# One PSUM bank for the attention sums, one more for projections, and Exps shared by heads, in a pre-LN block with sliding attention and GEGLU

## The chip, the cores and the metric

The kernel runs on one core of a Trainium2 chip. The metric is the device time of one execution in microseconds. Times come from runs on the chip; the profile is one execution that the hardware profiler recorded. Engines are named as the profile names them: PE is TensorE, PEld its weight loader, DVE VectorE, ACT ScalarE, POOL GpSimd, SP SyncE, which issues the DMAs. PSUM has eight banks of 128 x 512 f32; products are summed there and read out by DVE or ACT.

## The reference

One transformer block on 2048 tokens of 448 features: attention with 16 heads of 28 over a window of 256 tokens, then a gated feed-forward part of width 1792. All inputs are f32.

```python
h  = x + softmax(mask(q @ k.T * 28 ** -0.5)) @ v @ wo    # q, k, v = split(layernorm(x) @ wqkv)
h2 = h + (gelu(n @ w_gate) * (n @ w_up)) @ w_down        # n = layernorm(h)
# mask: 0 <= i - j < 256
```

## The kernel before

**Tiles and blocks.** Tokens are cut into 16 tiles of 128 and 4 chunks of 512 (c); heads into 4 groups of 4 (g). One attention block is B = 4c + g: 4 heads by 512 query tokens. Its keys are the chunk's four tiles and the two tiles before them (m = 0 to 5; for c = 0 only 2 to 5). A key tile m meets 1, 2 or 3 query tiles (`parts`): 1 for m = 0 and 5, 2 for m = 1 and 4, 3 for m = 2 and 3.

**Stages.** `ln1` normalises a tile and turns it, `values` (L570) and `project_tile` (L622) make v, q and k as sums of 11 products each, with the operands split into a high and a low part. q and k go to DRAM and come back (`loads`, L654) in the layout in which each query row can also carry its maximum. A block then runs four steps:

- `scores`: 16 products (L672), and on DVE the masked row maximum of each (L676), two instructions.
- `maxima`: twice a block, the maxima are turned by a product (L703) and copied by ACT into extra rows of q (L349).
- `probs`: for each head and key tile one product (L744), keys by queries with the maximum already subtracted, then one Exp on ACT (L748) into the tile `pp`; `select` (L759) clears the masked corners on POOL.
- `attend`: the value products (L778), four heads packed side by side, in two halves (key tiles 0 to 2, then 3 to 5), summed over all six key tiles in a bank that must be zero at the start; `drain` turns the sum out of that bank (L812), divides it and splits it; `output` (L835) multiplies by wo and adds to the residual.

`ln2` and `feed_forward` (L984, L1008) follow. The first four of the 56 feed-forward products, the first two of them under the name `early`, may run before attention is over.

**Banks.** `allowed` says which bank a kind of product may take. Before the change the banks are: 0 and 1 scores, 2 and 3 probability products and turned maxima, 4 and 5 the attention sums of even and odd blocks (`("att", B % 2)`), 6 and 7 layer norms, values, projections and `output`; 7 also helps scores and probabilities once no projections are left.

**What sets the order.** The kernel is planned when it is built. Each function hands operations to `Lists.op` with an engine, a cost, a latency and a key; `Lists.run` plays them on a model of the engines, picks on each engine the lowest key among those that could start about now, assigns banks, and emits the instructions in that order. The chip then runs each engine's instructions strictly in the emitted order, and waits on semaphores. So a key or a cost does not change any instruction, only its place; and an instruction that waits holds all that is behind it on its engine, DMAs on SP included. Keys are counted in units of a block's 16: block B's scores stand at 16 B + 4 i + j, its probabilities `LAG_P` later, its value products `LAG_V` after the last of those, its projections `EDGE` before it.

Of the kernel before, what the change touches and what calls it, by code (L numbers as in the profile page):

```python
# [21 lines left out]
SCALE = float(DH) ** -0.5  # L22
# [12 lines left out]
LAG_T = 6  # L35
LAG_P = 15
LAG_V = 12
EDGE = 9
WIN = 14
FFN = 1000  # L40
LEAD = 30
# [7 lines left out]
LN1 = (0, -19, 55, 134)  # L49
LN2 = (166, 224)  # L50
VKEY = (-30, -23, 14, 24)
VHALF = 0
FETCH = 170
# [173 lines left out]
def block_kernel(ctx: ExitStack, tc, x, wqk_in, wv_in, wo_in, ffn_in, out):  # L227
# [335 lines left out]
    def values(t, p, n):  # L563
        key = 64 * (t // 4) + VKEY[t % 4] if t > 3 else 8 * t - 37 if not p else VHALF + 6 * t
        b = Bank("v")
        w = slice(224 * p, 224 * (p + n))
        c = slice(128 * col(t), 128 * col(t) + 128)
        for a in range(NP):
            h, wb, xb = TERMS[a]
            op("pe", mm(224 * n), 0.29 if n == 1 else 0.38, key + a / 16, lambda a=a, h=h, wb=wb, xb=xb: nc.tensor.matmul(  # L570
                bank[b.k][:, 0:224 * n], xT[:, xb, c], wv[:, h, wb, w], start=(a == 0),
                stop=(a == NP - 1)), [XT(col(t)), *(WV(p + i, h, wb) for i in range(n))], () if a else [V(t, p, n)], b, tag="v")
        op("act", 0.29 if n == 1 else 0.47, 0.39 if n == 1 else 0.57, key + 1, lambda: to_hi(
            v[:, at_v(t), 8 * p:8 * (p + n), 0:DH], bank[b.k][:, 0:224 * n].rearrange("p (h d) -> p h d", d=DH)),
           ["ones"], [V(t, p, n)], b)
# [35 lines left out]
    def project_tile(c, m):  # L611
# [6 lines left out]
        base = 16 * B - EDGE  # L618
# [117 lines left out]
    def probs(B, m, j, o):  # L736
        u = B % 2
        lo, hi = parts(m)
        n = (hi - lo + 1) * 128
        b = Bank("prob")  # L740
        key = 16 * B + LAG_P + ORDER[m] + j * n / 384

        def one():
            nc.tensor.matmul(bank[b.k][:, 0:n], rk[u][0:104, j, m * 128:m * 128 + 128],  # L744
                             rq[u][0:104, j, lo * 128:(hi + 1) * 128], start=True, stop=True)

        def exp():
            nc.scalar.activation(pp[:, j, o * 128:o * 128 + n], bank[b.k][:, 0:n], AF.Exp, scale=SCALE)  # L748
        q = [("rk", u, m), *(("pick", u, j) for j in range(4)), *((w, u, i) for i in range(lo, hi + 1) for w in ("rq", "rx"))]
        op("pe", mm(n), 0.19 + n / 2400, key, one, q, (), b, tag="prob")  # L750
        op("act", 0.065 + n * 0.00088, 0.16 + n * 0.00088, key, exp, (), pp_at(o, hi - lo + 1, j), b, tag="exp")
# [16 lines left out]
    def attend(B, ms, at):  # L768
        g, c = block(B)
        b = acc.setdefault(B, Bank(("att", B % 2)))  # L770
# [161 lines left out]
    def feed_forward():  # L932
# [3 lines left out]
        for gi, gn in enumerate(GROUPS):  # L936
            for c in range(4):
                down = [Bank(("down", i)) for i in range(4)]
                for k in range(gn):
                    i = sum(GROUPS[:gi]) + k  # L940
                    while loaded < 2:
                        loaded += 1
                        split += 1
                        weights(loaded, 16 * NB + 5 * loaded if loaded < 2 else FFN + 30 * first[loaded] - 20)
# [158 lines left out]
    def clear():  # L1103
        for i in range(2):
            b = Bank(("att", i))
            op("dve", 0.4, 0.5, 12 + i, lambda b=b: nc.vector.memset(bank[b.k], 0.0), (), ["cleared"], b, tag="clear",
# [17 lines left out]
    for c in range(CS):  # L1124
# [12 lines left out]
        for g in range(NG):  # L1137
# [11 lines left out]
            for half in ((0, 1, 2), (3, 4, 5)) if c else ((2, 3), (4, 5)):  # L1149
                for m in half:  # L1150
                    for j in range(4):
                        probs(B, m, j, at[m])
# [18 lines left out]
    def allowed(kind):  # L1171
# [3 lines left out]
        if kind in ("ln1", "v", "proj", "task", "ln2"):  # L1175
            return [6, 7] + ([5, 4] if left["clear"] else []) + \
                ([3, 2] if L.fresh("prob") or not left["prob"] else []) + \
                ([1, 0] if L.fresh("score") or not left["score"] else []) + \
                ([4, 5] if kind == "task" and not left["att"] else [])
# [4 lines left out]
        if kind == "early":  # L1184
            return [] if left["proj"] or left["v"] else [6] + ([] if left["score"] else [0, 1]) + \
# [8 lines left out]
        what, i = kind  # L1194
        if what == "att":
            return [4 + i]
        return [] if left["att"] or left["task"] or left.get("early") else [4 + i]
# [68 lines left out]
```

## Time and profile before

| | us |
|---|---|
| median of 3 runs (lowest, highest) | 727.81 (727.71, 727.92) |
| the profiled execution's own time | 727.88 |
| its span, first to last instruction | 726.2 |
| first score starts at | 40.7 |
| last score starts at | 301.3 |
| feed-forward products from about 336 to | 720 |

The profile's page cuts the span into 40 slices; the digits are tenths busy:

```profile
PE   8999999999999999999999999999999999999997
DVE  7968779978787769658464313244133234232224
ACT  7738777777867787786453222244222223222221
POOL 5504743544354446741000000000000000000000
DMA  8896867888548984342732000012100000001002
```

Each column is 18.2 us. To about the 18th column attention runs and all engines have much to do; behind it PE alone is full. The chain by line names what the time went to:

```profile
PE bank L984 53%; PE bank L622 10%; PE bank L744 6%; PE bank L672 6%; PE bank L778 5%; PE bank L570 5%; PE bank L835 5%; PE bank L1008 3%; DMA hres<-in_x_dram 1%; PE bank L404 1%; DVE mt L676 1%; PE bank L703 0%; ACT pp L748 0%; DVE hres L1086 0%; ACT xT L349 0%
```

L984 is the feed-forward part; L622, L744, L672, L778, L570 and L835 are attention's products.

In a row of instruction groups stand: line, engine, operation, output<-input, partitions x elements, count, then busy us and the mean ns of one, then the idle time of the engine before them and what ended it. A row of waits reads: engine, waiting instruction <- the one that ended the wait: total us, number, longest. A row of the timeline: start, us, engine, line, operation, count; neighbours of one kind are merged.

### The profile page before, as it was taken

The numbers are of one execution on the slowest core, as the hardware profiler recorded it, in microseconds if no ns is written. First come the engines' busy times: TensorE is split into PE (matmuls) and PEld (weight loads), VectorE is DVE, ScalarE is ACT, GpSimd is POOL, SyncE is SP. The second block draws the span as 40 slices with busy tenths as digits, with TensorE's granted clock in tenths as the row PEclk, the third lists the DMA queues.
The fourth block names the chain that finished last, engine by engine and source line by source line (L and its number), as shares of the span: only waits on it lengthen the run. The fifth ranks groups of instructions, "written<-read, shape, count | busy, mean of one in ns | idle before, by whom it ended". The sixth has DMA issues, their size and how long they took to land.

```text
span 726.2 us, 15085 instructions
## 1 busy us (share of the span) xinstructions
PE 717.8 (99%) x5732; PEld 594.4 (82%) x5732; DVE 401.4 (55%) x1067; ACT 366.4 (50%) x927; POOL 162.6 (22%) x285
## 2 busy tenths in 40 slices
PE   8999999999999999999999999999999999999997
PEld 7887778878787877778888888888888888888886
DVE  7968779978787769658464313244133234232224
ACT  7738777777867787786453222244222223222221
POOL 5504743544354446741000000000000000000000
PEclk9999999999999999999999999999999999999999
DMA  8896867888548984342732000012100000001002
GB/s 308 268 311 211 234 159 203 214 255 207 161 122 241 242 234 136 77 112 42 203 105 84 1 2 1 1 44 83 42 1 2 1 1 1 2 1 51 19 34 102
DMA packets 96929, 82.06 MB, mean 113 GB/s; under 512 B 41736, under 2 KB 83016, under 8 KB 96840
## 3 DMA queue, kind: packets, MB, share of 16 engines
q1 hardware_dynamic: 96712, 80.98, 38.5%
q8 instruction: 45, 0.74, 0.4%
q14 instruction: 28, 0.23, 0.1%
q10 hardware_dynamic: 144, 0.11, 0.0%
HBM read 50.27 MB, written 31.03 MB: 112 GB/s over the span
## 4 chain that ended last, share of the span: by engine, by line
PE 94%; DVE 2%; ACT 1%; issue 1%; DMA 1%; POOL 0%; SPq 0%; DVEq 0%; POOLq 0%
PE bank L984 53%; PE bank L622 10%; PE bank L744 6%; PE bank L672 6%; PE bank L778 5%; PE bank L570 5%; PE bank L835 5%; PE bank L1008 3%; DMA hres<-in_x_dram 1%; PE bank L404 1%; DVE mt L676 1%; PE bank L703 0%; ACT pp L748 0%; DVE hres L1086 0%; ACT xT L349 0%
## 5 line engine op out<-in xcount | busy, mean ns | idle before, releaser
L676 DVE CUSTOM_DVE_ANT_0 mt<-bank,mt 128x384 bf16<-128x384 f32 (+2 forms) x256 | 126.8, 526 | 29.0 <-PE bank L672 27.2
L748 ACT ACTIVATE pp<-bank 128x384 f32<-128x384 f32 (+2 forms) x352 | 122.5, 388 | 39.8 <-PE bank L744 36.8
L1050 DVE TENSOR_TENSOR mt<-bank,mt 128x512 f32<-128x512 f32 x54 | 37.1, 688 | 143.3 <-ACT mt L1048 143.3
L759 POOL TENSOR_SCALAR_AFFINE_SELECT pp<-pp 128x512 f32<-128x512 f32 x120 | 75.9, 646 | 107.6 <-ACT pp L748 86.3
L744 PE MATMUL bank<-rq,rk 104*128 104x384 f32 (+2 forms) x352 | 97.6, 303 | 0.6 <-ACT pp L748 0.2
L622 PE MATMUL bank<-xT 128*128 128x512 f32 x308 | 94.9, 400 | 0.0
L1048 ACT ACTIVATE mt<-bank 128x512 f32<-128x512 f32 x54 | 32.2, 596 | 118.0 <-PE bank L984 118.0
L984 PE MATMUL bank<-xT,rk 64*128 64x512 f32 x656 | 82.0, 388 | 0.0
L984 PE MATMUL bank<-xT,rec 64*128 64x512 f32 x656 | 81.9, 388 | 0.0
L672 PE MATMUL bank<-rk,rq 84*128 84x384 f32 (+2 forms) x256 | 80.8, 346 | 0.8 <-DVE mx L676 0.5
L744 PEld LDWEIGHTS bank<-rq,rk 104*128 104x128 f32 x352 | 65.0, 189 | 17.4 <-ACT pp L748 5.9
L984 PEld LDWEIGHTS bank<-xT,rk 64*128 64x128 f32 x656 | 63.0, 184 | 12.2
L984 PEld LDWEIGHTS bank<-xT,rec 64*128 64x128 f32 x656 | 63.0, 184 | 12.1
L1086 DVE TENSOR_TENSOR hres<-bank,hres 128x448 f32<-128x448 f32 (+1 forms) x65 | 35.7, 611 | 66.9 <-PE bank L984 64.8
L990 ACT ACTIVATE e<-bank 1x1 f32<-1x1 f32 x162 | 25.7, 158 | 81.2 <-PE bank L984 80.5
L984 PE MATMUL bank<-xT,proj 64*128 64x512 f32 x533 | 66.6, 388 | 0.0
L622 PEld LDWEIGHTS bank<-xT 128*128 128x128 f32 x308 | 55.4, 189 | 7.4 <-ACT v L349 0.4
L984 PEld LDWEIGHTS bank<-xT,proj 64*128 64x128 f32 x533 | 51.1, 184 | 9.9
L672 PEld LDWEIGHTS bank<-rk,rq 84*128 84x128 f32 x256 | 46.3, 189 | 12.2 <-DVE mx L676 5.2
L570 PE MATMUL bank<-proj,xT 128*128 128x448 f32 (+1 forms) x220 | 51.0, 337 | 0.2 <-ACT v L349 0.2
L778 PE MATMUL bank<-pp,v 128*29 128x384 f32 (+2 forms) x704 | 45.4, 388 | 0.0
L349 ACT ACTIVATE rq<-bank 8x512 fp32r<-8x512 f32 x64 | 37.5, 586 | 13.6 <-PE bank L703 12.6
(147 smaller groups left out, 1088.5 us busy)
## 6 DMA issues: line engine op xcount, KB each, us to landing
rk<-k SPq DMA_DIRECT2D x44, 336.0 KB
rq<-q SPq DMA_DIRECT2D x32, 336.0 KB
v<-in_ffn_dram SPq DMA_DIRECT2D x7, 736.0 KB
q<-proj SPq DMA_DIRECT2D x11, 448.0 KB
raw<-in_ffn_dram SPq DMA_DIRECT2D x6, 736.0 KB
xn<-xn SPq DMA_DIRECT2D x72, 56.0 KB
xT<-xn SPq DMA_DIRECT2D x20, 192.0 KB
hres<-in_x_dram SPq DMA_DIRECT2D x16, 224.0 KB
```

Of the source, the lines that this page charges most:

```text
L349: nc.scalar.activation(dst, src, AF.Copy)
L570: op("pe", mm(224 * n), 0.29 if n == 1 else 0.38, key + a / 16, lambda a=a, h=h, wb=wb, xb=xb: nc.tensor.matmul(bank[b.k][:, 0:224 * n], x ...
L622: op("pe", mm(512) + 0.002, 0.403, key, lambda a=a, h=h, wb=wb, xb=xb: nc.tensor.matmul(bank[b.k], wqk[m][:, h, wb, :], xT[:, xb, cc * 128 ...
L672: nc.tensor.matmul(bank[b.k][:, o:384], rq[u][0:3 * DH, j, i * 128:i * 128 + 128], rk[u][0:3 * DH, j, m0 * 128:(i + 3) * 128], start=True, ...
L676: nc.vector.tensor_tensor_reduce(junk[s % 2][:, o:384], bank[b.k][:, o:384], mask[:, o:384], 1.0, -BIG, OP.add, OP.max, mx[i // 2][:, i % ...
L744: nc.tensor.matmul(bank[b.k][:, 0:n], rk[u][0:104, j, m * 128:m * 128 + 128], rq[u][0:104, j, lo * 128:(hi + 1) * 128], start=True, stop=True)
L748: nc.scalar.activation(pp[:, j, o * 128:o * 128 + n], bank[b.k][:, 0:n], AF.Exp, scale=SCALE)
L759: nc.gpsimd.affine_select(a, a, pattern=[[0, 4], [-cm, 128]], compare_op=op_, fill=0.0, base=0, channel_multiplier=cm)
L778: nc.tensor.matmul(bank[b.k][32 * j:32 * j + DH + 1, lo * 128:(hi + 1) * 128], v[:, at_v(4 * c - 2 + m), 4 * g + j, :], pp[:, j, at[m] * 1 ...
L835: op("pe", mm(D), 0.38, wk, lambda a=a, h=h, oh=oh, wh=wh, i=i, k=k: nc.tensor.matmul(bank[k.k][:, 0:D], ohl[:, h, oh, i * 128:(i + 1) * 1 ...
L984: nc.tensor.matmul(bank[bk.k][:, 0:n], w, m, start=bool(start), stop=bool(stop), tile_position=(64 * x, 0), skip_group_check=True)
L1050: op("dve", 0.605, 0.702, key + 2 * NP, lambda: nc.vector.tensor_tensor(blocks(g2), src(1), blocks(g2), op=OP.mult), [*G2, *held[1]], G2, ...
```

## The change

Four things are done.

- **Banks.** All blocks sum their attention in one bank, 4. Bank 5 goes to layer norms, values, projections, `output` and `early` feed-forward products, beside 6 and 7. Only one bank is cleared at the start.
- **Shared Exps.** `probs` works on a key tile instead of a head: as many heads as fit into 512 columns share a bank and one Exp: one head of 384 columns, two of 256, four of 128. The probability products themselves keep their sizes. The cost that the planner takes for them is now `G * (n / 2400 + 0.009)`, where `mm(n)` had a floor of 0.115.
- **Keys.** `LAG_V` 12 to 10, `EDGE` 9 to 8 and another 4 for the last chunk (`ELAST`), `LEAD` 30 to 10, `LN1` and `LN2` for one chunk each, `FETCH` 170 to 210, another table of keys for the values of the last tile group (`VLAST`); `WKEY` writes out two numbers that were computed before.
- **Order.** All engines' orders change from these.

```diff
 LAG_T = 6
+VLAST = (-30, -25, 14, 24)
+ELAST = 4
+WKEY = (256, 261)
 LAG_P = 15
-LAG_V = 12
-EDGE = 9
+LAG_V = 10
+EDGE = 8
-LEAD = 30
+LEAD = 10
-LN1 = (0, -19, 55, 134)
-LN2 = (166, 224)
+LN1 = (0, -19, 55, 128)
+LN2 = (166, 231)
-FETCH = 170
+FETCH = 210
...
-        base = 16 * B - EDGE
+        base = 16 * B - EDGE - (ELAST if c == 3 else 0)
...
-    def probs(B, m, j, o):
+    def probs(B, m, o):
         n = (hi - lo + 1) * 128
-        b = Bank("prob")
-        key = 16 * B + LAG_P + ORDER[m] + j * n / 384
-
-        def one():
-            nc.tensor.matmul(bank[b.k][:, 0:n], rk[u][0:104, j, m * 128:m * 128 + 128],
-                             rq[u][0:104, j, lo * 128:(hi + 1) * 128], start=True, stop=True)
-
-        def exp():
-            nc.scalar.activation(pp[:, j, o * 128:o * 128 + n], bank[b.k][:, 0:n], AF.Exp, scale=SCALE)
+        G = 512 // n
+        for j in range(0, 4, G):
+            b = Bank("prob")
+            key = 16 * B + LAG_P + ORDER[m] + j * n / 384
+
+            def some(j=j, b=b):
+                for i in range(G):
+                    nc.tensor.matmul(bank[b.k][:, n * i:n * i + n], rk[u][0:104, j + i, m * 128:m * 128 + 128],
+                                     rq[u][0:104, j + i, lo * 128:(hi + 1) * 128], start=True, stop=True)
+
+            def exp(j=j, b=b):
+                nc.scalar.activation(pp[:, j:j + G, o * 128:o * 128 + n],
+                                     bank[b.k][:, 0:G * n].rearrange("p (g t) -> p g t", g=G), AF.Exp, scale=SCALE)
...
+            cost = G * (n / 2400 + 0.009)
...
-        b = acc.setdefault(B, Bank(("att", B % 2)))
+        b = acc.setdefault(B, Bank("att"))
...
-        for i in range(2):
-            b = Bank(("att", i))
-            op("dve", 0.4, 0.5, 12 + i, lambda b=b: nc.vector.memset(bank[b.k], 0.0), (), ["cleared"], b, tag="clear",
+
+        b = Bank("att")
+        op("dve", 0.4, 0.5, 12, lambda b=b: nc.vector.memset(bank[b.k], 0.0), (), ["cleared"], b, tag="clear",
...
-            return [6, 7] + ([5, 4] if left["clear"] else []) + \
+            return [6, 7, 5] + ([4] if left["clear"] else []) + \
...
-            return [] if left["proj"] or left["v"] else [6] + ([] if left["score"] else [0, 1]) + \
+            return [] if left["proj"] or left["v"] else [6, 5] + ([] if left["score"] else [0, 1]) + \
...
+        if kind == "att":
+            return [4]
```

**Block 13's scores on PE.** In these rows bank_140 to bank_147 are banks 0 to 7; `rk,rq` are scores, `rq,rk` probability products, `ohl` products of `output`. In the middle of the block before the change:

```order
L744 MATMUL bank_142<-rq,rk 128x256
L672 MATMUL bank_147<-rk,rq 128x384
L835 MATMUL bank_146<-proj,ohl 128x448 x2
L744 MATMUL bank_143<-rq,rk 128x256
L744 MATMUL bank_142<-rq,rk 128x256
L672 MATMUL bank_140<-rk,rq 128x384
L835 MATMUL bank_146<-proj,ohl 128x448 x2
L672 MATMUL bank_141<-rk,rq 128x384
L744 MATMUL bank_143<-rq,rk 128x128
L672 MATMUL bank_147<-rk,rq 128x384
L744 MATMUL bank_142<-rq,rk 128x128
L835 MATMUL bank_146<-proj,ohl 128x448 x2
```

and after it, in the same block:

```order
L751 MATMUL bank_143<-rq,rk 128x256 x2
L846 MATMUL bank_146<-proj,ohl 128x448 x3
L675 MATMUL bank_140<-rk,rq 128x384
L846 MATMUL bank_146<-proj,ohl 128x448
L675 MATMUL bank_141<-rk,rq 128x384
L846 MATMUL bank_146<-proj,ohl 128x448
L751 MATMUL bank_142<-rq,rk 128x256 x2
L846 MATMUL bank_146<-proj,ohl 128x448
L675 MATMUL bank_140<-rk,rq 128x384
L751 MATMUL bank_143<-rq,rk 128x128 x4
L625 MATMUL bank_147<-xT 128x512
L675 MATMUL bank_141<-rk,rq 128x384
```

Before, four scores (three banks, 7 among them) stand in 12 rows and the whole block's 16 stand close; after, projections (L625) and values are still left to stand between them, scores keep to banks 0 and 1, and heads of one key tile stand together.

**ACT's Exps.** The Exps of key tiles 1 and 0 or 4 and 5 on ACT, in the middle of the program, before:

```order
L748 ACTIVATE pp<-bank_143 128x256
L748 ACTIVATE pp<-bank_142 128x256
L748 ACTIVATE pp<-bank_143 128x256
L748 ACTIVATE pp<-bank_142 128x128
L349 ACTIVATE raw<-bank_147 128x512
L748 ACTIVATE pp<-bank_143 128x128
L748 ACTIVATE pp<-bank_142 128x128
L748 ACTIVATE pp<-bank_143 128x128
L748 ACTIVATE pp<-bank_142 128x128
```

and after:

```order
L755 ACTIVATE pp<-bank_142 128x2x256
L755 ACTIVATE pp<-bank_143 128x2x256
L755 ACTIVATE pp<-bank_142 128x4x128
L352 ACTIVATE rq<-bank_142 8x4x128 x2
L352 ACTIVATE v<-bank_147 128x16x28
L755 ACTIVATE pp<-bank_143 128x4x128
L755 ACTIVATE pp<-bank_142 128x2x256
L755 ACTIVATE pp<-bank_143 128x2x256
```

Two or four Exps have become one, and other copies stand between fewer of them.

**SP's DMAs ahead of block 14.** Here the names carry the group and chunk: `k2_3` and `q2_3` are block 14's keys and queries in DRAM, `xn` tiles are turned tokens of `ln2`. Before:

```order
L654 DMA rk_68<-k1_3_106 84x4x256
L654 DMA rk_68<-k2_2_112 84x4x256
L447 DMA xT_66<-xn6_130 128x3x128
L449 DMA xT_66<-xn6_130 128x128
L447 DMA xT_66<-xn7_131 128x3x128
L449 DMA xT_66<-xn7_131 128x128
L632 DMA q3_3_121<-proj_69 112x2x512
L632 DMA k3_3_122<-proj_69 16x2x512
L654 DMA rq_67<-q2_3_113 84x4x256
L654 DMA rk_68<-k2_3_114 84x4x256
```

and after:

```order
L635 DMA k2_3_114<-raw_70 112x2x512
L635 DMA k3_3_122<-raw_70 16x2x512
L657 DMA rk_68<-k2_2_112 84x4x256
L637 DMA k2_3_114<-raw_70 112x512
L637 DMA k3_3_122<-raw_70 16x512
L448 DMA xn6_130<-xn1_74 32x14x32 x2
L657 DMA rq_67<-q2_3_113 84x4x256
L657 DMA rk_68<-k2_3_114 84x4x256
```

Before, the writes of block 14's keys stand 22 rows and more ahead of the load that reads them; after, four and seven rows ahead of it.

More of the change, by code (lines that the diff above doesn't have):

```diff
@@ L563, in values @@
     def values(t, p, n):
-        key = 64 * (t // 4) + VKEY[t % 4] if t > 3 else 8 * t - 37 if not p else VHALF + 6 * t
+        key = 64 * (t // 4) + (VKEY if t < 12 else VLAST)[t % 4] if t > 3 else 8 * t - 37 if not p else VHALF + 6 * t
         b = Bank("v")
@@ L739, in probs @@
         n = (hi - lo + 1) * 128
-        b = Bank("prob")
-        key = 16 * B + LAG_P + ORDER[m] + j * n / 384
-        def one():
-            nc.tensor.matmul(bank[b.k][:, 0:n], rk[u][0:104, j, m * 128:m * 128 + 128],
-                             rq[u][0:104, j, lo * 128:(hi + 1) * 128], start=True, stop=True)
-        def exp():
[L748 to L751, printed above, removed]
+        G = 512 // n
[9 more added lines that the diff above has]
+                                     bank[b.k][:, 0:G * n].rearrange("p (g t) -> p g t", g=G), AF.Exp, scale=SCALE)
+            q = [("rk", u, m), *(("pick", u, i) for i in range(4)),
+                 *((w, u, i) for i in range(lo, hi + 1) for w in ("rq", "rx"))]
+            cost = G * (n / 2400 + 0.009)
+            op("pe", cost, cost + 0.17, key, some, q, (), b, tag="prob")
+            op("act", 0.065 + G * n * 0.00088, 0.16 + G * n * 0.00088, key, exp, (),
+               [p for i in range(G) for p in pp_at(o, hi - lo + 1, j + i)], b, tag="exp")
     def select(B, m, o):
@@ L943, in feed_forward @@
                         split += 1
-                        weights(loaded, 16 * NB + 5 * loaded if loaded < 2 else FFN + 30 * first[loaded] - 20)
+                        weights(loaded, WKEY[loaded] if loaded < 2 else FFN + 30 * first[loaded] - 20)
                     if n == PAIRED:
@@ L1150, in block_kernel @@
                 for m in half:
-                    for j in range(4):
-                        probs(B, m, j, at[m])
+                    probs(B, m, at[m])
                     select(B, m, at[m])
@@ L1175, in allowed @@
         if kind in ("ln1", "v", "proj", "task", "ln2"):
-            return [6, 7] + ([5, 4] if left["clear"] else []) + \
+            return [6, 7, 5] + ([4] if left["clear"] else []) + \
                 ([3, 2] if L.fresh("prob") or not left["prob"] else []) + \
                 ([1, 0] if L.fresh("score") or not left["score"] else []) + \
-                ([4, 5] if kind == "task" and not left["att"] else [])
+                ([4] if kind == "task" and not left["att"] else [])
         if kind == "score":
@@ L1193, in allowed @@
             return ([] if left["score"] else [0, 1]) + ([] if left["prob"] else [2, 3])
[L1194 to L1197, printed above, removed]
+        if kind == "att":
+            return [4]
+        return [] if left["att"] or left["task"] or left.get("early") else [4 + kind[1]]
     def idle(t, until, bank_free):
```

## The prediction

> **What bounds the kernel now.** I read the page first: the span, the busy shares and the chain of work that ended last.
>
> ```profile
> span 726.2 us, 15085 instructions
> PE 717.8 (99%) x5732; PEld 594.4 (82%) x5732; DVE 401.4 (55%) x1067; ACT 366.4 (50%) x927; POOL 162.6 (22%) x285
> PE 94%; DVE 2%; ACT 1%; issue 1%; DMA 1%; POOL 0%; SPq 0%; DVEq 0%; POOLq 0%
> ```
>
> TensorE carries 94% of the chain. Its order is fixed when the program is built, so the kernel gets shorter only if its products shrink or if it stops less between them. Where it stops is seen from the busy time of each engine by stage: attention (20 to 336 us), the feed-forward part behind it, and the 20 us in which block 13 of the 16 attention blocks is scored.
>
> ```profile
> 20.00:336.00 316.00, 313.84 (x2114) 248.39 (x2112) 250.31 (x810) 236.94 (x585) 147.15 (x243) 1.00 0.69 193
> 336.00:720.00 384.00, 384.00 (x3507) 328.65 (x3507) 133.36 (x221) 113.32 (x318) 3.26 (x8) 1.00 0.12 37
> 262.00:282.00 20.00, 19.71 (x128) 14.41 (x128) 19.75 (x70) 16.78 (x46) 9.96 (x15) 1.00 0.55 175
> ```
>
> The columns are PE, PEld, DVE, ACT, POOL, granted clock, DMA share and GB/s. The clock is 1.00 everywhere. The feed-forward part has no gap that this view can show (384.00 of 384.00), and its products stay as they are: I carry its 384 us over unchanged. In attention the PE column is flattering, since the ends of products are modelled; the weight loader is the better witness, so I read what it waited for between 20 and 336 us (total, number, longest).
>
> ```profile
> PEld bank L778 <- issue: 11.5, 52, 0.4
> PEld bank L744 <- ACT pp L748: 5.9, 22, 0.6
> PEld bank L672 <- DVE mx L676: 5.2, 13, 0.8
> PEld bank L744 <- ACT rq L349: 1.3, 6, 0.4
> PEld bank L778 <- POOL pp L759: 1.3, 5, 0.4
> ```
>
> The first row is the packed value product itself (L778): 52 gaps of 0.2 us, in which nothing is awaited. The same products run in the changed kernel, so this stays. What a change of order can win is in the other rows: 13.7 us of waits of a probability product (L744) for the Exp that empties its bank, of a score (L672) for the maximum that empties its bank, and of two smaller kinds.
>
> **The change, part by part.** *Products.* Their number and sizes are the same; four 128-wide heads now follow each other into one bank. Does a run of short products cost more than the same products spread among long ones?
>
> ```profile
> 158.91 0.36 PE L835 MATMUL bank<-wos,ohl 128*128 128x448 f32 x1
> 159.11 0.34 PE L744 MATMUL bank<-rq,rk 104*128 104x384 f32 x1
> ...
> 163.56 0.28 PE L744 MATMUL bank<-rq,rk 104*128 104x256 f32 x1
> 163.68 0.37 PE L835 MATMUL bank<-wos,ohl 128*128 128x448 f32 x1
> ...
> 164.42 0.39 PE L622 MATMUL bank<-xT 128*128 128x512 f32 x1
> 164.66 0.22 PE L744 MATMUL bank<-rq,rk 104*128 104x128 f32 x1
> 164.72 0.45 PE L622 MATMUL bank<-xT 128*128 128x512 f32 x1
> 165.00 0.22 PE L744 MATMUL bank<-rq,rk 104*128 104x128 f32 x1
> 21.77 0.44 PE bank L404 x4
> ```
>
> From start to start a 448-wide product takes 0.20 us, one of 256 takes 0.12 and one of 512 before a short one 0.24. The short one takes 0.06, but the long one behind it 0.28: the weights of the long one were not yet in. So a lone short product costs about 0.06 + 0.04 = 0.10 us, and four 128-wide ones in a row take 0.44 (the transposes of L404, from the chain), 0.11 each. 28 runs of four, at 0 to 0.01 us a product, make 0 to 1.1 us; I take **0**, the isolated cost being read to 0.01 only.
>
> *Shared Exps.* 352 Exps become 212: 128 of one head, 56 of two heads (256 wide), 28 of four (128 wide).
>
> ```profile
> L748 ACT ACTIVATE pp<-bank 128x384 f32<-128x384 f32 x128 | 56.5, 490 | 9.1 <-PE bank L744 8.5 <-PE bank L672 0.3
> L748 ACT ACTIVATE pp<-bank 128x256 f32<-128x256 f32 x112 | 39.5, 382 | 13.9 <-PE bank L744 12.8
> L748 ACT ACTIVATE pp<-bank 128x128 f32<-128x128 f32 x112 | 27.9, 278 | 16.8 <-PE bank L744 15.5
> L349 ACT ACTIVATE proj<-bank 128x512 fp32r<-128x512 f32 x18 | 10.8, 601 | 3.3 <-issue 2.1 <-PE bank L622 1.2
> ```
>
> An Exp gets 0.106 us longer with each 128 columns, so one of 512 is about 0.60 us, as the 512-wide copy is (601). The busy sum falls from 39.5 + 27.9 = 67.4 to at most 84 x 0.60 = 50.4: **17 us of ScalarE**, all beside TensorE, so none of it counts by itself. What counts is the 5.9 us that TensorE waited for Exps. There are 0.6 times as many hand-overs of these banks, which alone gives 0.6 x 5.9 = 3.5; and while a pair (2 x 0.12) or four (0.44) fill one bank, the other is emptied for longer than the 0.06 to 0.18 us that a lone product gives. So I take 2.4 left, a gain of **3.5**. Ends: all 5.9 goes; or every one of the 22 waits becomes as long as the longest, 0.6, which is 13.2 and a loss of 7.3.
>
> [...]
>
> *Where the scores stand.* The new key table spreads block 13, as the first excerpt of order shows.
>
> ```profile
> 262.00 0.51 PE L672 MATMUL bank<-rk,rq 84*128 84x384 f32 x2
> 269.46 0.34 PE L672 MATMUL bank<-rk,rq 84*128 84x384 f32 x1
> 269.64 0.22 PE L744 MATMUL bank<-rq,rk 104*128 104x128 f32 x1
> 270.72 0.92 PE L672 MATMUL bank<-rk,rq 84*128 84x384 f32 x2
> 284.70 0.55 DVE L676 CUSTOM_DVE_ANT_0 mt<-bank,mt 128x384 bf16<-128x384 f32 x1
> 285.18 0.55 DVE L676 CUSTOM_DVE_ANT_0 mt<-bank,mt 128x384 bf16<-128x384 f32 x1
> ...
> L838 DVE TENSOR_TENSOR hres<-bank,hres 128x448 f32<-128x448 f32 x32 | 19.9, 621 | 12.7 <-PE bank L835 10.6 <-PE bank L744 2.1
> L817 DVE STREAM_TRANSPOSE oT<-oblk 128x512 f32<-128x512 f32 x16 | 11.3, 707 | 0.0
> ```
>
> From its first score (262.00) to its last (the second of 270.72) pass about 9.2 us. TensorE's work there, counted in the order: 18 products 384 wide at 0.18 (269.46 to 269.64), 4 of 256, 4 of 128 at 0.11, 6 of 448 and the value products of half a block (1.4 of the 1.50 in the next fence) make 6.8. VectorE's: 15 maxima at 0.48 (284.70 to 285.18) are 7.2, and six other instructions, an addition (0.62), a transpose (0.71), two splits no longer than these and two small ones, about 2. So VectorE sets this stretch, as its 19.75 of 20.00 said, and TensorE loses 2.4 us. In the new order the same count gives TensorE 15.9 (23 of 384, 13 of 512, 21 of 448, 6 of 256, 8 of 128, a whole block's value products) against some 10.4 of VectorE, by the same prices: that loss goes. It comes back in part in block 15: there 8.7 of TensorE stand against 8.5 of VectorE now, and 7.8 against 9.4 then, 1.6 us short. Net **-0.8**. Ends: -2.4 (block 15 hides behind what it waits for anyway) and +1.6 (nothing gained at 13, all paid at 15).
>
> *One attention bank.* The next block's first value product now waits until the transpose has emptied the bank.
>
> ```profile
> 150.09 1.50 PE L778 MATMUL bank<-pp,v 128*29 128x384 f32 x24
> 151.66 0.72 DVE L812 STREAM_TRANSPOSE oblk<-bank 128x512 f32<-128x512 f32 x1
> 161.16 1.50 PE L778 MATMUL bank<-pp,v 128*29 128x128 f32 x24
> ```
>
> The transpose follows the last value product by 0.07 us and takes 0.72; the next block's first comes 9 us later. In the new order a half block of probability products always lies between the two, so I take **0**. Without that cover each of 15 hand-overs costs the transpose's 0.72, 10.8 us, with scores and projections queued behind it on TensorE. The second clear of a bank, one 0.4 us memset, also goes, beside other work. The earlier attention (LAG_V 10) touches the 1.3 us of waits for the selects; in the new order more products lie between a half's last probability product and its value products: **-0.5** (0 to -1.3).
>
> *Moved maxima.* The second transposed maximum of block 14 is now followed directly by a probability product that needs it.
>
> ```profile
> 283.75 0.25 PE L703 MATMUL bank<-one,mhl 128*72 128x128 f32 x1 [0.50 <-DVE mhl L696]
> 284.03 1.18 ACT L349 ACTIVATE rq<-bank 8x512 fp32r<-8x512 f32 x2 [0.26 <-PE bank L703]
> ```
>
> From such a transpose to the end of its first copy (half of 1.18) pass 0.28 + 0.59, about 0.9 us: **+0.9** there (0 if a filler's start is late anyway, 1.5 if both copies are awaited).
>
> *Moved projections.* EDGE, ELAST and the key tables bring the last chunk's projections close to their use: for block 14, 100 products between the last of its projection and its first score instead of 200, for block 11, 109 instead of 312. In between lie two copies, the DMAs to DRAM and the loads back; the third excerpt shows these DMAs, now side by side on SP's queue, where a write that is late holds every later load.
>
> ```profile
> 14.35 5.00 PE bank L622 x22
> 40.72 0.34 PE L672 MATMUL bank<-rk,rq 84*128 84x128 f32 x2
> SPq L654 <- PE bank L744: 41.6, 18, 8.8
> ```
>
> Now the loads wait for their buffer (41.6 us of SP's waits end with a probability product), not for a projection. A chain from projection to score stands alone only at the start: 19.35 to 40.72, 21.4 us, among the first loads of everything. The new distance for block 14 is 16 us of products (10 of 512, 29 of 448, 20 of 384, 8 of 256, 8 of 128, one attention). Two 0.6 us copies and two DMA trips should take less than that when DMA is half idle (0.55 above), so I take **+0.5**; ends 0 and, with the start's 21.4, 5.4 at block 14 and about 4 each at 11 and 15, 13 in all.
>
> The other keys (LN1, LN2, VLAST, WKEY, FETCH, LEAD), and the early feed-forward product in bank 5, only reorder work that lies under TensorE's: 0.
>
> **The sum.** 0 - 3.5 - 0.8 + 0 - 0.5 + 0.9 + 0.5 = -3.4 us. The profiled execution took 727.88 us (726.2 of span, 1.7 around it), 0.07 above the median of 727.81. So 727.88 - 3.4 = **724.5 us**.
>
> **The rivals.** *No change:* a static order passes a removed wait on to the next shared thing. For it: VectorE is full where block 13 is scored and a shared Exp frees its bank later. Against: the waits sit in different places. It gives 727.5. *More than forecast:* all waits for Exps, selects and the whole loss of block 13 vanish: 5.9 + 1.3 + 2.4 = 9.6 less, 718.3. For it: longer hand-over distances in all 16 blocks. *Late projections, slower:* if the chain takes over 16 us, the score of block 14 waits, and all behind it on TensorE; at the start's 21.4 the three places cost 13, less 3.4 of gains: 737; at 19, some 6: 730. For it: writes and loads are neighbours on SP. Against: the start's chain had DMA at its busiest. *One attention bank, slower:* if the transpose is queued behind VectorE's maxima by more than the products between, up to 10.8 comes on top; with two thirds of it, about 732.
>
> [...]
>
> **How the numbers follow.** A measurement of this kernel can tell about 0.2%, 1.5 us, from no change. Forecast (1.5 to 6 us faster): 0.48; more than that: 0.11; no change: 0.19; late projections: 0.13; attention bank or slower shared Exps: 0.09. So faster 0.59, same 0.19, slower 0.22. The range goes from 718.3, the large gain, to 730.5, just above the mild late projection; what is left out is the full price of either slower case. The forecast's own range is 722 to 726.3.
>
> **What would show it.** In the changed profile: waits of the probability product for Exps near 2.4 us in fewer than 22 stops; VectorE no longer full over 20 us around block 13, but near full at the last block; no wait of a value product for the transpose; ScalarE's Exps near 50 us busy; scores with no idle time ended by a DMA. It would be wrong if a loader's wait for rq or rk loads appears, or if waits for Exps keep their sum.

## The result and the profile after

| | before | after |
|---|---|---|
| median, us (lowest, highest) | 727.84 (727.48, 727.92; 6 runs) | 723.21 (722.44, 724.28; 6 runs) |
| the profiled execution's own time | 727.88 | 722.63 |
| its span | 726.2 | 720.9 |

The ratio is 0.9939 with a 95% interval of 0.9927 to 0.9951: 4.6 us faster, 5.25 us between the two profiled executions. The six runs after lie in two groups, 722.44 to 722.63 and 723.79 to 724.28, where the six of before lie in one; that comes up again below.

The head of the page of the changed kernel:

```profile
span 720.9 us, 14938 instructions
PE 711.7 (99%) x5732; PEld 594.8 (83%) x5732; DVE 398.2 (55%) x1066; ACT 353.0 (49%) x787; POOL 163.1 (23%) x285
PE 88%; ACT 3%; DVE 2%; DMA 2%; issue 1%; SPq 1%; POOL 1%; DVEq 0%; ACTq 0%; POOLq 0%
```

The 5732 products are all there, and ScalarE has 140 instructions fewer. TensorE is 99% busy in both pages, so this line shows no gain. Nor does the smaller share of PE in the chain (94% before, 88% after) show a loss: from 199 to 209 us the chain now runs over SP's queue and a DMA, and between 197 and 215 us TensorE is still busy 17.93 of 18.00. Where the chain reaches the feed-forward part tells more. Its rows for the feed-forward part, first of the kernel before, then of the one after (start, us, what):

```profile
336.10 383.58 PE bank L984 x3504
```

```profile
330.33 25.63 PE bank L995 x233
...
360.90 353.31 PE bank L995 x3226
```

The feed-forward part starts 5.8 us earlier (336.10 to 330.33) and ends 5.5 us earlier (719.68 to 714.21): the gain lies in attention, and about 0.3 is given back behind it. So the loader's waits between 20 us and the end of attention are the view to compare (total, number, longest):

```profile
PEld bank L789 <- issue: 11.2, 49, 0.4
PEld bank L751 <- ACT rq L352: 3.2, 6, 1.6
PEld bank L751 <- ACT pp L755: 2.9, 9, 0.7
PEld bank L675 <- DVE mx L679: 2.7, 6, 0.6
...
PEld bank L789 <- POOL pp L770: 1.2, 5, 0.3
...
PEld bank L675 <- DMA rq<-q: 0.2, 1, 0.2
```

L751, L675 and L789 are the former L744, L672 and L778. Waits of probability products for Exps fell from 5.9 us in 22 stops to 2.9 in 9, waits of scores for maxima from 5.2 in 13 to 2.7 in 6. One kind grew: probability products that wait for the copied maxima (`rq`), from 1.3 to 3.2, and half of it is a single wait of 1.6.

### The profile page after: what moved, and what is told of

Same layout as the page of the kernel before. It is cut to its first block, busy times and chain, and to the rows that moved or that the text cites. A ratio compares the mean times of both kernels' runs of the same rounds, so it can differ in the third digit from the quotient of the medians.

```text
span 720.9 us, 14938 instructions
## 1 busy us (share of the span) xinstructions
PE 711.7 (99%) x5732; PEld 594.8 (83%) x5732; DVE 398.2 (55%) x1066; ACT 353.0 (49%) x787; POOL 163.1 (23%) x285
## 4 chain that ended last, share of the span: by engine, by line
PE 88%; ACT 3%; DVE 2%; DMA 2%; issue 1%; SPq 1%; POOL 1%; DVEq 0%; ACTq 0%; POOLq 0%
PE bank L995 53%; PE bank L625 8%; PE bank L751 6%; PE bank L675 5%; PE bank L789 5%; PE bank L573 4%; PE bank L846 4%; PE bank L1019 2%; DMA hres<-in_x_dram 1%; ACT pp L755 1%; DMA rk<-k 1%; PE bank L407 1%; ACT xT L352 1%; ACT rq L352 0%; DMA q<-proj 0%
## 5 line engine op out<-in xcount | busy, mean ns | idle before, releaser
L755 ACT ACTIVATE pp<-bank 128x384 f32<-128x384 f32 (+1 forms) x212 | 105.8, 534 | 34.5 <-PE bank L751 25.7
L625 PE MATMUL bank<-xT 128*128 128x512 f32 x308 | 96.0, 399 | 0.0
L751 PE MATMUL bank<-rq,rk 104*128 104x384 f32 (+2 forms) x352 | 82.3, 303 | 2.1 <-ACT rq L352 1.5
L675 PE MATMUL bank<-rk,rq 84*128 84x384 f32 (+2 forms) x256 | 81.2, 342 | 0.0
L751 PEld LDWEIGHTS bank<-rq,rk 104*128 104x128 f32 x352 | 60.0, 190 | 14.4 <-ACT rq L352 3.2
L625 PEld LDWEIGHTS bank<-xT 128*128 128x128 f32 x308 | 56.0, 189 | 7.0 <-ACT v L352 0.4
L995 PEld LDWEIGHTS bank<-xT,proj 64*128 64x128 f32 x533 | 51.1, 184 | 10.4 <-ACT e L1001 0.6
L675 PEld LDWEIGHTS bank<-rk,rq 84*128 84x128 f32 x256 | 46.6, 189 | 11.8 <-DVE mx L679 2.7
L789 PE MATMUL bank<-pp,v 128*29 128x384 f32 (+2 forms) x704 | 45.4, 388 | 0.0
```

The lines of the kernel that those rows point to most:

```text
L625: op("pe", mm(512) + 0.002, 0.403, key, lambda a=a, h=h, wb=wb, xb=xb: nc.tensor.matmul(bank[b.k], wqk[m][:, h, wb, :], xT[:, xb, cc * 128 ...
L675: nc.tensor.matmul(bank[b.k][:, o:384], rq[u][0:3 * DH, j, i * 128:i * 128 + 128], rk[u][0:3 * DH, j, m0 * 128:(i + 3) * 128], start=True, ...
L751: nc.tensor.matmul(bank[b.k][:, n * i:n * i + n], rk[u][0:104, j + i, m * 128:m * 128 + 128], rq[u][0:104, j + i, lo * 128:(hi + 1) * 128] ...
L755: nc.scalar.activation(pp[:, j:j + G, o * 128:o * 128 + n], bank[b.k][:, 0:G * n].rearrange("p (g t) -> p g t", g=G), AF.Exp, scale=SCALE)
L789: nc.tensor.matmul(bank[b.k][32 * j:32 * j + DH + 1, lo * 128:(hi + 1) * 128], v[:, at_v(4 * c - 2 + m), 4 * g + j, :], pp[:, j, at[m] * 1 ...
L995: nc.tensor.matmul(bank[bk.k][:, 0:n], w, m, start=bool(start), stop=bool(stop), tile_position=(64 * x, 0), skip_group_check=True)
```

## The experiments

Twelve kernels ran. Times are medians, beside the kernel before on the same chip (727.71 to 727.88).

### Shared Exps alone, with the order held

The plan of after stands; only what one operation issues is changed.

```diff
-                nc.scalar.activation(pp[:, j:j + G, o * 128:o * 128 + n],
-                                     bank[b.k][:, 0:G * n].rearrange("p (g t) -> p g t", g=G), AF.Exp, scale=SCALE)
+                for i in range(G):
+                    nc.scalar.activation(pp[:, j + i, o * 128:o * 128 + n], bank[b.k][:, n * i:n * i + n], AF.Exp,
+                                         scale=SCALE)
```

> The kernel after with the same banks, keys and order of products; only each shared Exp is issued as two or four Exps of one head on the same bank (ScalarE about 17 us busier, a bank is emptied later by 0.2 us for a pair and 0.5 us for four). Theory 1 (the shared Exp itself is what shortens the waits for Exps): 2 to 4 us slower than after, 725 to 727, and the waits of the probability products for Exps go from about 3 us back to 6 or more. Rival (the gain lies in order and banks; ScalarE is not saturated, smaller Exps cost nothing): within 0.7 us of after, 722.5 to 724, and the waits stay near 3 us.

Measured: 725.26 us, ratio to before 0.9967 (0.9954 to 0.9979), so 2.05 us slower than after. The loader's waits between 20 and 333 us:

```profile
PEld bank L751 <- ACT pp L756: 5.0, 14, 0.8
PEld bank L751 <- ACT rq L352: 4.1, 7, 2.2
```

Waits for Exps went from 2.9 to 5.0 us, a little under the 6 that were expected, and waits for the copied maxima from 3.2 to 4.1. The order is held, so it is the shared Exp itself that shortens them: theory 1 in direction, and by the medians in size. The time is less than these 3 us of waits. TensorE at block 14 of s1, and the busy time by stretch behind it (the eighth column is the granted clock):

```profile
287.53 0.28 PE L706 MATMUL bank<-one,mhl 128*72 128x128 f32 x1
289.90 1.30 PE L751 MATMUL bank<-rq,rk 104*128 104x384 f32 x3 [2.09 <-ACT rq L352]
```

```profile
290.50:294.00 3.50, 3.50 (x10) 2.74 (x10) 0.13 (x1) 2.81 (x6) 2.64 (x4) 0.51 0.38 66
```

In after the same two rows start at 287.06 and 288.83. So up to block 14 the split Exps cost 0.47 us, with its stop 1.07, and the feed-forward part starts 2.5 later (332.83 against 330.33). The other 1.4 lie behind that stop, where s1 has a stretch of half clock and the profiled run of after has none. Against the three runs of after with a mean clock below 1.000 (median 724.23), s1 is 1.0 us slower. ScalarE is 7.8 us busier than in after (360.8 to 353.0), not the 17 that were expected.

### One part of the change at a time, and two at a time

Each part was put into the kernel before by itself, then in pairs; the order is planned anew each time. The edits are the hunks of the diff above: *sharing* (`probs` and its call), *banks* (`attend`, `clear`, `allowed`), *keys* (the tables, `ELAST`, `VLAST`, `WKEY`).

> The kernel before with one part of the change: heads share a bank and an Exp; banks of attention and keys as before. The order is planned anew. Theory 1 (shared Exps are worth about 3.5 us by themselves): 723.5 to 725.5. Rival (the keys and bank 5 make the gain): 727 to 728.5, with the stretch in which block 13 is scored still full on VectorE.

> The kernel before with one attention bank instead of two and the other given to projections and early feed-forward products; probability products, Exps and keys as before. Theory 1 (one attention bank costs nothing, and nothing waits for a projection's bank): 727 to 728.5. Rival (the additional projection bank is what gains): 723 to 726. Second rival (the hand-over of the one bank is paid): 730 or more, with waits of value products for the transpose.

> The kernel before with the changed key tables only (VLAST, ELAST, WKEY, LAG_V, EDGE, LEAD, LN1, LN2, FETCH). Theory 1 (the tables spread block 13 and bring the attention earlier, 0.8 + 0.5 us, less 1 to 1.5 of new waits): 726.5 to 728.5. Rival (the tables carry the gain): 723 to 725. Second rival (the tables only fit the new banks and bring late projections here): 730 or more, with waits for loads.

> The kernel after with one part undone: each head has its own bank use and its own Exp, as before; banks and keys as after; the order is planned anew. Theory 1 (shared Exps are worth some 2 to 3.5 us, the rest of the gain lies in banks and keys together): 725 to 727.5. Rival (the three parts only pay together, since the keys were found for all three): 728 to 732, as with each part alone.

> The kernel before with shared Exps and the new banks, keys as before; planned anew. Theory 1 (the gain is that of an order that fits, and each part apart fits worse: none of the pairs keeps the gain): 727 to 731. Rival (shared Exps and bank 5 make the gain, the keys trim it): 723.5 to 725.5, without the full VectorE at block 13.

> The kernel before with shared Exps and the new keys, two attention banks as before; planned anew. Theory 1 (none of the pairs keeps the gain): 727 to 732. Rival (keys that spread block 13 and shared Exps suffice, the banks give nothing): 723 to 725.5.

The last two columns are sums over all rows of the loader's waits between 20 and 340 us, by the engine that ended them, in one profiled execution of each kernel.

| parts of the change | us | ratio to before (95%) | waits ended by ScalarE | by VectorE |
|---|---|---|---|---|
| none (before) | 727.84 | | 12.6 | 8.7 |
| sharing | 729.33 | 1.0023 (1.0013, 1.0033) | 8.8 | 12.1 |
| banks | 731.30 | 1.0055 (1.0041, 1.0069) | 18.2 | 6.1 |
| keys | 732.62 | 1.0069 (1.0056, 1.0082) | 14.2 | 7.1 |
| banks and keys | 732.60 | 1.0065 (1.0052, 1.0077) | 18.2 | 6.6 |
| sharing and keys | 730.06 | 1.0031 (1.0019, 1.0042) | 12.5 | 8.8 |
| sharing and banks | 724.78 | 0.9963 (0.9949, 0.9976) | 8.8 | 8.1 |
| all three (after) | 723.21 | 0.9939 (0.9927, 0.9951) | 10.9 | 6.6 |

No part pays alone: +1.6, +3.6 and +4.9 us against the kernel before on the same chip, but -4.6 together. Only the two rows with sharing *and* banks are faster than before. Theory 1 missed for sharing alone (723.5 to 725.5), banks alone (727 to 728.5), keys alone (726.5 to 728.5), banks with keys (725 to 727.5) and sharing with banks (727 to 731); it held for sharing with keys (727 to 732). The rival of sharing alone (727 to 728.5) missed too, and that of banks with keys (728 to 732) by 0.6. The second rivals of banks and of keys had the time but not the cause: no value product waits for the transpose in the one; in the other no wait of the loader ends with a DMA, and one product waits 0.2 us for a load. For sharing with banks the rival had the time (723.5 to 725.5), though scores still wait 4.8 us for maxima there.

The two columns say part of why. In each of four pairs that differ by the banks alone, VectorE's column falls (8.7 to 6.1, 12.1 to 8.1, 7.1 to 6.6, 8.8 to 6.6). With a third bank, projections spread the scores, and VectorE keeps up. But without sharing ScalarE's column rises with it (12.6 to 18.2, 14.2 to 18.2); the likely reason, not tested by itself, is that the copies of those projections now stand in its queue among the Exps. In each of the four pairs that differ by sharing, ScalarE's column falls (12.6 to 8.8, 18.2 to 8.8, 14.2 to 12.5, 18.2 to 10.9). The rows of banks alone show where its load comes out, among them a first feed-forward product (L1008) behind the copied maxima:

```profile
PEld bank L744 <- ACT pp L748: 6.6, 22, 0.8
PEld bank L744 <- ACT rq L349: 3.3, 9, 0.8
PEld bank L1008 <- ACT rq L349: 2.4, 1, 2.4
```

So the bank moves waits from VectorE to ScalarE, and the shared Exps take them from ScalarE. One execution per plan stands behind each sum, and a new plan reshuffles everything, so single entries are good to a microsecond or so, and the smallest of these steps (7.1 to 6.6) is within that; it is the same direction in all four pairs that carries this.

The times follow the sum of the two columns in five of the seven rows, once the stretches of half clock are counted (about 1.7 us each, see below; the profiled runs of sharing alone, of sharing with banks and of banks with keys have one each, the second by its mean clock of 0.998). Against before, sharing has 0.4 us less of waits and one such stretch (measured +1.6), banks 3.0 more (+3.6), banks with keys 3.5 more and a stretch (+4.7), sharing with banks 4.4 less and a stretch (-3.0), all three 3.8 less (-4.6). So, by these figures, sharing alone is slower by its half clock, not by its waits, which only passed from ScalarE to VectorE. Keys alone and sharing with keys have 21.3 us, as before, and no such stretch, and are 4.9 and 2.3 us slower; what the keys cost with two attention banks stays open.

### The new stop at block 14

In after the longest stop stands where the prediction put a small loss: the second turned maximum of block 14 and the probability products behind it. The timeline of TensorE and ScalarE there:

```profile
287.04 0.31 ACT L352 ACTIVATE lasthi<-xT 64x128 fp32r<-64x128 f32 x1
287.06 0.28 PE L706 MATMUL bank<-one,mhl 128*72 128x128 f32 x1
287.38 0.31 ACT L352 ACTIVATE xT<-xT 64x128 fp32r<-64x128 f32 x1
287.59 0.57 ACT L755 ACTIVATE pp<-bank 128x512 f32<-128x512 f32 x1
288.19 1.20 ACT L352 ACTIVATE rq<-bank 8x512 fp32r<-8x512 f32 x2
...
288.83 0.62 PE L751 MATMUL bank<-rq,rk 104*128 104x384 f32 x2 [1.49 <-ACT rq L352]
```

The turned maximum ends at 287.34; its first copy starts 0.85 us later, behind the split of a transposed tile and an Exp. Four kernels take this apart with the plan held. Operations of the plan are named by their number in it: 2545 the value products of block 13, 2551 the turned maximum, 2548 and 2550 the split (ScalarE) and its subtractions (VectorE).

```diff
             self.order.append(o)
-            o.fn()
+            i = len(self.order) - 1
+            if i in late:
+                held.append((late[i], o))
+            else:
+                o.fn()
+            for _, h in [h for h in held if h[0] == i]:
+                h.fn()
...
+        late = {2545: 2551}                              # s2
+        late = {2548: 2596, 2550: 2596}                  # s3
+        late = {2545: 2551, 2548: 2596, 2550: 2596}      # s4
+        late = {2545: 2551, 2548: 2596, 2550: 2614}      # s5
```

> The kernel after, same plan and banks; only the second turned maximum of block 14 (L706) now stands on TensorE ahead of the value products of block 13's last half (24 products, 1.5 us) instead of behind them. Theory 1 (the 1.7 us stall behind it is set by ScalarE's queue: Exp, split of a transposed tile, Exp, and only then the two copies of the turned maximum): the stall shrinks by at most 0.3 us, the time stays within 0.6 us of after. Rival (the stall is set by where the turned maximum stands on TensorE): 1.2 to 1.6 us faster than after.

> The kernel after, same plan and banks; only the split of one transposed tile at block 14 (three ScalarE copies, 1.2 us, and the two VectorE subtractions behind them) is issued some 4 us later, behind the Exps that follow. Theory 1 (ScalarE's queue sets the stall): the copies of the turned maximum start at most 0.3 us behind it instead of 0.85, the stall of 1.7 us falls to about 0.8, 0.6 to 1 us faster than after. Rival (place on TensorE sets it): within 0.3 us of after.

> The kernel after with both moves of the two runs ahead of this one: turned maximum ahead of the value products, split of the tile behind the Exps. Theory 1: the copies then run beside the value products, the stall falls to 0.5 or less, 1.2 to 1.7 us faster than after (about 721 to 722 where after has 722.5). Rival: no more than the better of the two moves alone.

> The kernel after with both moves of s4_both, and the two VectorE subtractions of the moved split now behind the six maxima that they held up there (a new stop of 2.3 us in s4_both). [...] Rival 1 (the windows of half clock come whatever the stops are): still two groups, 1.5 us apart. Rival 2 (a planned order passes the wait on to the next shared engine, as in s3 and s4): 722.3 or more, with a new stop.

Measured: 722.71, 724.82, 724.80 and 722.68 us, with ratios to before of 0.9934 (0.9922 to 0.9946), 0.9960 (0.9948 to 0.9972), 0.9960 (0.9948 to 0.9973) and 0.9931 (0.9919 to 0.9944). The longest of TensorE's own waits between 284 and 300 us, for these four in turn:

```profile
PE bank L758 <- ACT rq L359: 0.9, 1, 0.9
PE bank L713 <- ACT pp L762: 0.5, 1, 0.5
```

```profile
PE bank L682 <- DVE mx L686: 1.8, 1, 1.8
PE bank L758 <- ACT rq L359: 0.7, 1, 0.7
```

```profile
PE bank L682 <- DVE mx L686: 2.1, 1, 2.1
```

```profile
PE bank L682 <- DVE mx L686: 1.2, 1, 1.2
```

ScalarE's queue does set the stop: moving the turned maximum alone (s2) leaves 0.5 + 0.9 of 1.5, both ended by ScalarE, moving the split (s3) cuts it to 0.7, both (s4) leave no wait for `rq`. But no time is won; s3 and s4 are 1.6 us slower than after, and their profiled runs, at mean clocks of 0.995 and 0.997, have two and one stretches of half clock. The split's two subtractions, 1.5 us on VectorE, came later with it, and a score (L682) then waits for a maximum that stands behind them: 1.8 to 2.1 us, still 1.2 where six maxima were put ahead of them (s5). The expectations of s3, 0.6 to 1 us faster, and of s4, 1.2 to 1.7 us faster, fell, and of s5 the second rival held: the wait went to the next shared engine. Between 284 and 300 us ScalarE and VectorE both have to hand something to TensorE at every step, and a move of the split changes which of the two is late. No version here is faster than after beyond its interval.

### Windows of half clock

The traces hold the TensorE clock that was granted. In some executions it is 0.50 for one stretch of about 3.4 us within attention, a window of half clock: in s1 it reads 0.63 from 290 to 292 us, 0.51 from 292 to 294 and 1.00 in the 2 us on either side, in sharing alone 0.52 from 288 to 290, 0.63 from 290 to 292 and 1.00 on either side. Both come to 1.7 us of clock lost. Such a stretch was there in the profiled runs of sharing alone, banks with keys, and s1, s3 (twice) and s4, and by its mean clock of 0.998 in that of sharing with banks, behind a long stop (2.09 us in s1) or several shorter ones (in sharing alone TensorE is busy 5.26 of 6.00 us from 282 to 288). Before is not free of it either, by its mean clock: its slowest runs on three of the chips, 728.44 to 728.56 us, have 0.997. One kernel puts stops of rising length where nothing else waits.

```diff
-        op("act", 0.485 + table, 0.608 + table, key + NP, lambda: nc.scalar.activation(
-            blocks(g2), src(0), AF.Gelu_apprx_tanh), held[0], G2, bs[0], after=exps)
+        again = {12: 6, 16: 7, 20: 8, 24: 9, 28: 10, 32: 11, 36: 12, 40: 13}.get(n, 0)
+
+        def gelu():
+            for _ in range(1 + again):
+                nc.scalar.activation(blocks(g2), src(0), AF.Gelu_apprx_tanh)
+        op("act", 0.485 + table, 0.608 + table, key + NP, gelu, held[0], G2, bs[0], after=exps)
```

> The kernel after, same plan; in the feed-forward part, at eight places some 29 us apart, the Gelu of one group is done 6, 7, 8 and so on to 13 more times over with the same result (0.6 us each on ScalarE), so that TensorE stops for lengths that rise by 0.6 us from place to place, from nothing to 4 us and more. [...] Rival (the windows of half clock in the other runs have to do with attention's load, not with stops): the clock stays at 1.00 behind all eight stops.

Measured: 767.58 us, ratio 1.0547 (1.0533 to 1.0561), mean clock 0.977 to 0.980. That is 44 us more; the eight stops come to 30.9 us, from 1.29 to 7.2 each. Three of the eight places in the timeline of TensorE, with the wait in brackets:

```profile
407.09 2.80 PE L995 MATMUL bank<-xT,rk 64*128 64x512 f32 x21 [1.29 <-ACT e L1001]
```

```profile
438.20 2.12 PE L995 MATMUL bank<-xT,rk 64*128 64x512 f32 x16 [1.92 <-ACT e L1001]
```

```profile
469.95 3.54 PE L995 MATMUL bank<-xT,rk 64*128 64x512 f32 x20 [2.55 <-ACT e L1001]
```

The busy time by stretch behind them (the eighth column, before the DMA share, is the granted clock):

```profile
409.00:420.00 11.00, 11.00 (x102) 9.38 (x101) 4.89 (x8) 2.83 (x7) 0.00 (x0) 1.00 0.01 1
437.00:444.00 7.00, 5.80 (x52) 4.91 (x54) 3.34 (x7) 1.60 (x5) 0.00 (x0) 1.00 0.00 0
...
471.30:474.70 3.40, 3.40 (x20) 2.77 (x18) 0.00 (x0) 0.60 (x1) 0.00 (x0) 0.50 0.00 0
```

Behind the stops of 1.29 and 1.92 us the clock stays at 1.00; behind that of 2.55 it reads 0.50 from 471.30 to 474.70 and 1.00 from there to 482, so the rival fell. What follows each of the five longer stops is not shown. By an estimate from the mean clock of 0.977 over the span of 766.5 us, if all else was at 1.00, the run had some 35 us at half clock, some ten such stretches.

The same run repeats the stop of block 14 unchanged, 1.49 us long as in after. In h1 it lasts from 287.11 to 288.60, and half clock follows:

```profile
287.00:290.30 3.30, 1.60 (x6) 0.78 (x5) 2.54 (x5) 3.18 (x8) 2.08 (x4) 1.00 0.36 74
290.40:293.70 3.30, 3.30 (x10) 3.01 (x10) 0.35 (x1) 2.69 (x6) 2.38 (x4) 0.50 0.41 70
```

against after's own profiled run, where it lasts from 287.34 to 288.83 and none follows:

```profile
288.00:291.30 3.30, 2.26 (x8) 1.39 (x9) 1.77 (x5) 3.20 (x8) 2.49 (x3) 1.00 0.44 88
291.40:294.70 3.30, 3.30 (x23) 2.97 (x25) 2.37 (x9) 3.30 (x8) 2.45 (x7) 1.00 0.33 61
```

So half clock follows the same stop in one execution and not in the other; what decides it was not shown. It fits the two groups of after's times: 722.44 to 722.63 at a mean clock of 1.000, 723.79 to 724.28 at 0.996 to 0.998, 1.6 us apart where one stretch costs 1.7. Only profiled executions show where a stretch lies; that the three longer runs had theirs behind block 14 is inferred from these two traces.

## Why the prediction was right, and where not

The forecast was 724.5 us, a gain of 3.4; the median came out at 723.21, inside the forecast's own range of 722 to 726.3. The steps:

- **What bounds it:** right. The gain is in the waits of the loader in attention; the feed-forward part kept its time within 0.3 us.
- **Products, 0:** too low, and past its upper end of 1.1. In after a run of four takes 0.39 to 0.43 us from its first start to the next product's (78.03 to 78.42) in 19 of the 26 runs that the timeline shows whole, and 0.50 in the other seven (298.19 to 298.69). Most are followed by a product that takes 0.05 to 0.07 us longer than elsewhere (298.69 to 298.92, 0.23 where 0.18 was read). So a run costs at least 0.45 against 0.40 for four lone ones: 1.4 us or more for 28 runs.

```profile
78.03 0.56 PE L751 MATMUL bank<-rq,rk 104*128 104x128 f32 x4
78.42 0.45 PE L625 MATMUL bank<-xT 128*128 128x512 f32 x1
...
298.19 0.66 PE L751 MATMUL bank<-rq,rk 104*128 104x128 f32 x4
298.69 0.39 PE L675 MATMUL bank<-rk,rq 84*128 84x384 f32 x1
298.92 0.57 PE L846 MATMUL bank<-wos,ohl 128*128 128x448 f32 x2
```

- **Shared Exps, -3.5:** mechanism right, size too large. 84 shared Exps took 596 ns each, 48.5 us where at most 50.4 was said; 2.9 us of waits in 9 stops stand where 2.4 in fewer than 22 were said. The working took a wait of the loader for lost time, one to one; with the order held, sharing is worth 1.0 us without the half clock and 2.05 with it. That stretch is in s1's profiled run (0.51 from 290.50 to 294.00) and, by their mean clock of 0.996 to 0.998, in all five of its runs, in after in three of six.

```profile
L755 ACT ACTIVATE pp<-bank 128x512 f32<-128x512 f32 x84 | 48.5, 596 | 13.1 <-PE bank L751 11.4 <-PE bank L789 0.3
```

  ScalarE is not saturated over attention (busy 223.04 us of the 310.00 from 20 to 330 in after), yet smaller Exps cost 1.0 to 2.05 us. At block 14, where TensorE waits for it, ScalarE is busy 3.20 of 3.30 us.
- **Scores of block 13, -0.8:** right place, too small. Block 13's 16 scores now start between 249.8 and 266.3 us, over 16.5 us; before it was 9.2, from 262.0 to 271.2. No score waits for VectorE there, which is busy 11.83 of 17.00 us (10.4 was counted):

```profile
249.60:266.60 17.00, 17.00 (x126) 13.91 (x125) 11.83 (x41) 11.20 (x22) 7.91 (x13) 1.00 0.82 224
```

  The stretch from 262 to 282 us, in which VectorE was full before, now holds the end of block 13's scores and all of block 14's. No score waits for a maximum in it any more (1.9 us in 6 stops before), and TensorE does 142 products instead of 128:

```profile
262.00:282.00 20.00, 19.86 (x142) 16.42 (x141) 18.60 (x69) 14.70 (x29) 12.47 (x22) 1.00 0.89 241
```

  VectorE's waits over attention fell by 2.1 us (8.7 to 6.6). The loss expected at block 15, with VectorE near full, did not come. Its scores start between 292.0 and 300.5 us (291.3 to 301.3 before) and wait 0.9 us for VectorE in 2 stops, 1.0 in 2 before. The stretch in before, then in after:

```profile
291.00:302.00 11.00, 10.52 (x78) 7.64 (x70) 10.21 (x36) 9.07 (x22) 10.67 (x17) 1.00 0.25 61
```

```profile
291.00:302.00 11.00, 10.90 (x91) 8.17 (x89) 8.81 (x33) 8.09 (x19) 8.24 (x12) 1.00 0.19 42
```

- **One attention bank, 0:** right. No value product waits for the transpose. The shortest time from a transpose's end to the next block's first value product is 2.05 us, at block 4:

```profile
133.46 0.71 DVE L823 STREAM_TRANSPOSE oblk<-bank 128x512 f32<-128x512 f32 x1
136.22 1.18 PE L789 MATMUL bank<-pp,v 128*29 128x128 f32 x20
```

- **Earlier attention, -0.5:** nothing came of it; waits for selects are 1.2 us in 5 stops, 1.3 in 5 before.
- **Turned maximum of block 14, +0.9:** mis-sized as well. The working counted the product and the first of its two copies as if ScalarE were free. That copy starts 0.85 us late, and the stop is 1.5. This meets the upper end of 1.5, but not by its reason, a wait for both copies: the probability product starts at 288.83, after the first. Waits for `rq` rose by 1.9 in all, and three of the six runs pay about another 1.6 us in clock.
- **Late projections, +0.5:** one wait of 0.2 us for a load. Such a wait was named as a sign of being wrong, but at this size it changes nothing; the rival of 730 and more is out. (The products counted for block 14's distance come to 15.1 us by the prediction's own prices, not 16.)
- **The sum** treated the parts as independent, and that they are not: alone each is a loss, and only sharing with banks is a gain. It could hold because it was read from the order of the finished kernel, in which all three are present. That it came within 1.3 us is partly luck: Exps, runs of four and copied maxima came out worse than their terms, while VectorE's waits fell by 2.1 instead of 0.8 and gaps without a wait, which were put at nothing, by 1.4. The rival *no change* named what the rows of sharing and of banks alone show, a wait that passes to the next shared engine.

By rows of waits the gain of 5.25 between the profiled executions divides into VectorE -2.1, ScalarE -1.7 (Exps -3.0, copied maxima +1.9, others the rest), gaps without a wait -1.4 (16.7 to 15.3 over all rows ended by issue), POOL +0.5 and DMAs +0.2. That is -4.5; the remainder was not traced, and the s1 run shows that a wait of the loader need not cost its whole length.

## What to carry to other kernels

When several engines feed a busy TensorE in a fixed order, taking load from one of them pays only as far as the next one keeps up (here sharing alone is 1.6 us slower, with the banks 3.0 faster); test such edits together as well as alone, and read the waits by the engine that ends them. A stop should be priced with what stands ahead of the awaited instruction in its own engine's queue, 0.85 us at block 14. And a new stop, here of 1.5 us, can cost more than its length, in some executions and not in others: half clock, 1.7 us of work, follows it in the profiled run of h1 and not in that of after.

## What the runs showed of the hardware

The clock was not expected to matter: in before it was 1.00 in attention and in the feed-forward part. In several of these runs TensorE's granted clock fell to 0.50 for a stretch of about 3.4 us, and three of the six runs of after, at a mean clock of 0.996 to 0.998 instead of 1.000, took about 1.6 us more. Half clock came behind a stop of 2.55 us in h1's feed-forward part, of 2.09 in s1, and of 1.49 with one of 0.21 behind it at h1's block 14. It did not come behind stops of 1.29 and 1.92 in h1, of the same 1.49 and 0.21 in the profiled run of after, or of 2.1 in the kernel with the banks alone, where TensorE is busy 7.89 of 10.00 us from 320 to 330 and the clock reads 1.00 from 320 to 340. So the length of the stop is not all that counts. Nor does it take a stop of that kind: in banks with keys TensorE is busy 5.77 of 6.00 us from 246 to 252, and the clock reads 0.83 from 250 to 252 and 0.50 from 252 to 254. What the clock goes by was not shown.
